# A kernel of attention and two expert stages: the products of packed keys for both halves of the heads, at one place in y

## The chip, the cores and the metric

The kernel runs on one core of a Trainium2 chip. Its engines are TensorE (PE: matmuls and their weight loads), VectorE (DVE), ScalarE (ACT), GpSimd (POOL) and SyncE (SP, which here issues the DMAs); each runs its own instructions in order and they wait for each other by semaphores. The metric is the device time of one execution in microseconds (us), as the median of runs.

## What is computed

Three steps follow one another; the third is the longest, and the change lies in the second.

```python
p_packed = sm_attn(p, k, v)                  # 8 batches, 8 heads, 32 packed queries, 576 keys of 64
x = sm_attn(q, p_packed, p_packed)           # 576 queries against the 32 packed rows
...
h = np.maximum(np.maximum(x @ w1, x @ w2), x @ w3)   # 4608 tokens, 512 -> 768
x2 = h @ w_out                                       # 768 -> 512
...
h = x2 @ w_in                                # 512 -> 2048, then P(h) / Q(h), elementwise
out = g @ w_out2                             # 2048 -> 512
```

## The kernel before

The kernel never forms x. Since x is the attention weights of a query (32 per head) times the packed rows, x @ w is those weights times (packed rows @ w), and the small products m = packed rows @ w are what the change moves.

The batches are worked in four batch pairs, bp0 to bp3. Each has a y-phase and an x2-phase:

- **y-phase.** Six slices f of the 768 hidden columns, 128 each, and two batches b2: `y_stage` (L462 ff.) makes three w-steps, one for each of w1, w2, w3, of 12 matmuls of 128 x 288. The first is copied out of PSUM by ACT (L471), the other two are joined with it by a max on DVE (L473). So a batch pair has 36 w-steps, counted here 0 to 35. After each, `between()` is called, which issues whatever else goes on beside y.
- **m.** `m_stage(bp, g, mt)` makes the products of one half g of the heads (four heads of each of two batches) with the columns of slice f + 1: eight matmuls of 32 output rows and 384 columns (L321) into one PSUM tile pst, a copy by ACT (L325) that gives the high part, and, in the function that it returns, a subtraction on DVE (L326) that gives the low part. It takes the next weight tile wt and, by `again(n)`, issues the DMA that fills another with a later piece of the same weights from the scratch w_scr. Both halves are needed when y comes to slice f + 1.
- **x2-phase.** Eight `x2_stage`, four output slices m of two batches: 36 matmuls into a PSUM tile psy, whose copy out is made by ACT (m under 3) or DVE (L489), and a store.
- **Weights.** They come packed in 64 bits and are decoded piece by piece (`Feed`): a load of w_raw on SP (L104), DVE L76, L82, ACT L83, L84, DVE L87, L91, L96, and POOL L99, which writes the wt tile; then a store of the decoded piece from SP to a scratch. In bp0 these are w1 to w3 and w_out; in bp1 to bp3 the weights of the third step.
- **Next batch pair.** Its attention (`Ahead`; scores S, transposes T, values V, scaling Z, query side s) runs in between, spread over the w-steps by the table PACK and over the x2-phase by SECOND, which holds the first slice's m.

Buffers that bind: two PSUM tiles pst (m, T, V and Z share them), two psy, four wt, three w_raw, one dec_r, and one pair of m tiles for even and one for odd slices.

The order of the instructions on each engine is made by a list scheduler: it has a simulated timeline and takes, engine by engine, the first instruction in the program's order whose inputs it holds for ready. So instructions can move ahead of the place where the code issues them, and one edit can change the order far from it. A few decode steps keep the program's order. The third step (moe2) follows after bp3.

Of the kernel before, what the change touches and what calls it, by code (L numbers as in the profile page):

```python
# [33 lines left out]
def attn_moe_moe2_kernel(  # L34
# [177 lines left out]
    def next_wt():  # L212

        n = next(used)
        wt = wt_ready.pop(n)
        n += NWT
        return wt, (n if NW <= n < NBP * NW else None)

    def again(n):
        if n is not None:  # L220
            wt = wt_tile().rearrange("p a b -> p (a b)")[:, :768]
            nc.sync.dma_start(wt, w_scr[n // 2 % 6, n % 2])
            wt_ready[n] = wt
# [21 lines left out]
    def load_w2(tiles, o, n):  # L245

        for x in range(2):
            nc.sync.dma_start(tiles[:, x].bitcast(F32), w2_scr[:, x, 512 * o : 512 * (o + n)])
# [58 lines left out]
    def m_tiles(f):  # L307

        return [mp[f % 2].tile([128, 2, 2, 384], F32R, name=f"m{x}") for x in "hl"]

    def m_stage(bp, g, mt):

        ps = ps_t.tile([128, 2, 512], F32, name="pst")
        wt, n = next_wt()
        for b2 in range(2):
            for h in range(4):
                i, j = divmod(h, 2)
                l, c = slice(64 * j, 64 * j + 64), 32 * (h ^ b2)  # L320
                pe.matmul(ps[c : c + 32, b2, :384], lhsT=ppk[l, bp % 2, 2 * g + b2, 32 * h : 32 * h + 32],  # L321
                          rhs=wt[l, 384 * i : 384 * i + 384], start=True, stop=True)
        again(n)
        hi, lo = (t[:, :, g, :] for t in mt)
        act.copy(hi, ps[:, :, :384])  # L325
        return lambda: dve.tensor_tensor(out=lo, in0=ps[:, :, :384], in1=hi.bitcast(F32), op=ALU.subtract)  # L326
# [132 lines left out]
    def y_stage(b2, f, m, a2, between, lo_eng):  # L459
        hm = hx.tile([128, 2, 288], F32, name="hm")  # L460
        mh, ml = m
        for w in range(3):  # L462
            ps = ps_y.tile([128, 2, 512], F32, name="psy")
            for half in range(2):
                for g in range(2):
                    ah, al = a2[g]
                    c = slice(288 * half, 288 * half + 288)
                    mm3(ps[:, half, :288], mh[:, g, 128 * w : 128 * w + 128], ml[:, g, 128 * w : 128 * w + 128],
                        ah[:, c], al[:, c], g == 0, g == 1)
            if w == 0:  # L470
              act.copy(hm, ps[:, :, :288])  # L471
            else:
              dve.tensor_tensor(out=hm, in0=ps[:, :, :288], in1=hm, op=ALU.max)  # L473
            between()
        hh = hp_pool.tile([128, S], F32R, name=f"hh{b2}{f}")
        hl = hp_pool.tile([128, S], F32R, name=f"hl{b2}{f}")
        split(hh, hl, hm.rearrange("p a b -> p (a b)"), lo_eng=lo_eng)
        return hh, hl
# [13 lines left out]
    def wi_at(f):  # L492

        if f < 1:
            return wi_0
        return wi_b[:, :, f - 1]
# [36 lines left out]
    for bp in range(NBP):  # L533
# [20 lines left out]
        for f in range(6):  # L554
            if f < 5:
                nmt = m_tiles(f + 1)

            def between(bp=bp, f=f, now=now):
                t = next(turn)
                if now.soft:  # L560
                    now.do("g")
                if f < 5 and t % 6 in (2, 4):
                    m_stage(bp, t % 6 // 2 - 1, nmt)()
                if t >= 2:
                    next(pack, None)
                if bp == 0:
                    if t % 3 < 2 and t < 32:
                        feed.half_step()
                elif t in y_steps[bp]:
                    feed2.step()  # L570

            if bp == NBP - 1 and f == 2:
                load_w2(wi_at(0), 0, 1)
            for b2 in range(2):
                hs[b2][f] = y_stage(b2, f, [t[:, b2] for t in mt], a2[b2], between,
                                    "dve" if bp == 0 or (b2, f) == (1, 5) else "pool")
            mt = nmt
# [109 lines left out]
    f = NQA  # L687
# [65 lines left out]
```

## Time and profile before

| | us |
|---|---|
| median of 3 runs | 1391.42 (1391.15 to 1391.81) |
| span of the profiled execution | 1386.2 |
| y-phase of bp0, from its first matmuls, and x2-phase | to 160.4, to 205.5 |
| bp1: y-phase, x2-phase | 85.1, 49.6 |
| bp2: y-phase, x2-phase | 85.2, 57.1 |
| bp3: y-phase, x2-phase | 67.5, 39.3 |
| moe2 | from 589.3 to the end |

The span is that of one profiled execution; it lies 5.2 us under the median of the runs, which have the start and the end of the execution around it. The page gives TensorE as busy for 1308.8 us (94% of the span), VectorE for 1055.0 and ScalarE for 802.8. The page's chain is read from the end back; the timelines give each instruction's start and duration, and in brackets how long its engine was idle before it and what ended that. PEclk is the granted clock of TensorE as a share of 2.4 GHz.

### The profile page before, as it was taken

The page shows a single profiled execution, that of the slowest core. Times are in us where ns is not written, and L with a number is a line of the kernel's source. Part 1 is how long each engine was busy: PE and PEld are TensorE (multiplying, and loading weights), DVE is VectorE, ACT ScalarE, POOL GpSimd, SP SyncE. Part 2 cuts the span into 40 slices and gives each one's busy share as a digit, 9 for nine tenths or more (in the row PEclk, how much of TensorE's full clock was granted, in tenths as well). Part 3 has the DMA queues.
Part 4 walks back from the last instruction along what each step waited for, and adds up shares of the span by engine and source line. Part 5 has one row for each costly group of instructions (what it writes and reads, how often), then busy time and mean ns, then how long its engine had stood idle before and what let it go on. Part 6 is the DMA issues. An engine that isn't in the chain of part 4 may idle for free.

```text
span 1386.2 us, 21521 instructions
## 1 busy us (share of the span) xinstructions
PE 1308.8 (94%) x8496; PEld 1089.6 (79%) x8496; DVE 1055.0 (76%) x1634; ACT 802.8 (58%) x1337; POOL 235.4 (17%) x226
## 2 busy tenths in 40 slices
PE   4488999999998899999999999999999999999998
PEld 2277787779777889988888888888888888888886
DVE  4698766677667764188888978889888888888887
ACT  2355534443443342276866867668677686776765
POOL 2332253334333533000100101001010010100000
PEclk8599999999999999999999999999999999999999
DMA  8567546666654731960100101001010010010000
GB/s 278 182 203 257 182 140 197 211 207 218 191 186 142 238 100 59 329 258 1 61 1 3 60 1 49 12 1 61 1 38 24 0 54 0 16 38 1 31 0 31
DMA packets 51557, 140.86 MB, mean 102 GB/s; under 512 B 5632, under 2 KB 5632, under 8 KB 50688
## 3 DMA queue, kind: packets, MB, share of 16 engines
q1 hardware_dynamic: 51168, 138.96, 30.2%
q8 instruction: 67, 1.10, 0.3%
q10 hardware_dynamic: 288, 0.52, 0.1%
q14 instruction: 34, 0.28, 0.1%
HBM read 99.09 MB, written 40.37 MB: 101 GB/s over the span
## 4 chain that ended last, share of the span: by engine, by line
PE 79%; DVE 7%; DMA 3%; ACT 2%; issue 2%; POOL 1%; SPq 0%; POOLq 0%; ACTq 0%; DVEq 0%
PE po L61 10%; PE po L62 10%; PE po L63 10%; PE psh L62 9%; PE psh L61 9%; PE psh L63 9%; PE psy L61 7%; PE psy L63 6%; PE psy L62 6%; PE pst L321 2%; DMA w_scr<-wt 1%; POOL wt L99 1%; DVE hm L473 1%; DMA w_raw<-in_w_dram 1%; DVE wt L91 1%
## 5 line engine op out<-in xcount | busy, mean ns | idle before, releaser
L61 PE MATMUL po<-wq_b,gh 128*128 128x512 f32 x540 | 212.3, 393 | 0.8 <-ACT gh L54 0.8
L62 PE MATMUL po<-wq_b,gh 128*128 128x512 f32 x540 | 211.3, 391 | 0.0
L62 PE MATMUL psh<-xl,wi_b 128*128 128x512 f32 x540 | 211.0, 391 | 0.0
L63 PE MATMUL psh<-xh,wi_b 128*128 128x512 f32 x540 | 210.6, 390 | 0.0
L61 PE MATMUL psh<-xh,wi_b 128*128 128x512 f32 x540 | 210.6, 390 | 0.0
L652 ACT ACTIVATE hb<-psh,babs 128x512 f32<-128x512 f32 (+1 forms) x145 | 100.1, 690 | 188.9 <-PE psh L63 188.9
L61 PE MATMUL psy<-a2h,mh 128*128 128x288 f32 x576 | 180.3, 313 | 11.5 <-DVE hm L473 6.1
L655 DVE SCALAR_TENSOR_TENSOR hb<-h,babs,hb 128x512 f32<-128x512 f32 (+1 forms) x145 | 108.3, 747 | 97.7 <-ACT h L653 97.5
L63 PE MATMUL po<-wq_b,gl 128*128 128x512 f32 x540 | 181.7, 391 | 0.0
L63 PE MATMUL psy<-a2h,ml 128*128 128x288 f32 x576 | 171.2, 298 | 4.6 <-DVE ml L326 4.6
L62 PE MATMUL psy<-a2l,mh 128*128 128x288 f32 x576 | 171.5, 298 | 0.0
L58 POOL TENSOR_TENSOR xl<-xr,xh 128x512 fp32r<-128x512 f32 x28 | 36.5, 1304 | 632.3 <-ACT xh L54 632.3
L61 PEld LDWEIGHTS psy<-a2h,mh 128*128 128x128 f32 x576 | 109.6, 190 | 36.2 <-DVE hm L473 11.2
L61 PE MATMUL psy<-hh,wo_h 128*128 128x288 f32 x384 | 117.6, 306 | 9.7 <-ACT hm L489 9.3
L63 PEld LDWEIGHTS po<-wq_b,gl 128*128 128x128 f32 x540 | 101.3, 188 | 24.0
L61 PEld LDWEIGHTS po<-wq_b,gh 128*128 128x128 f32 x540 | 101.4, 188 | 22.9 <-ACT gh L54 1.2
L62 PEld LDWEIGHTS po<-wq_b,gh 128*128 128x128 f32 x540 | 101.4, 188 | 22.4
L61 PEld LDWEIGHTS psh<-xh,wi_b 128*128 128x128 f32 x540 | 101.4, 188 | 22.1
L62 PEld LDWEIGHTS psh<-xl,wi_b 128*128 128x128 f32 x540 | 101.4, 188 | 21.7
L63 PEld LDWEIGHTS psh<-xh,wi_b 128*128 128x128 f32 x540 | 101.4, 188 | 21.7
L62 PE MATMUL psy<-hl,wo_h 128*128 128x288 f32 x384 | 115.8, 301 | 0.0
L63 PE MATMUL psy<-hh,wo_l 128*128 128x288 f32 x384 | 115.6, 301 | 0.0
(105 smaller groups left out, 2765.3 us busy)
## 6 DMA issues: line engine op xcount, KB each, us to landing
w_raw<-in_w_dram SPq DMA_DIRECT2D x32, 512.0 KB, 4.0
w_scr<-wt SPq DMA_DIRECT2D x32, 512.0 KB, 4.9
wt<-w_scr SPq DMA_DIRECT2D x36, 384.0 KB, 4.1
kt<-in_k_dram SPq DMA_DIRECT2D x16, 576.0 KB, 5.6
vraw<-in_v_dram SPq DMA_DIRECT2D x16, 576.0 KB, 6.6
kt<-in_q_dram SPq DMA_DIRECT2D x16, 576.0 KB, 5.6
w_raw<-in_w_dram SPq DMA_DIRECT2D x12, 768.0 KB, 5.6
x_scr<-hm SPq DMA_DIRECT2D x32, 288.0 KB, 4.1
```

What stands on the lines that cost most here:

```text
L58: e.tensor_tensor(out=lo, in0=src, in1=hi.bitcast(F32), op=ALU.subtract)
L61: pe.matmul(out_ap, lhsT=lh, rhs=rh, start=first, stop=False)
L62: pe.matmul(out_ap, lhsT=lh, rhs=rl, start=False, stop=False)
L63: pe.matmul(out_ap, lhsT=ll, rhs=rh, start=False, stop=last)
L91: dve.scalar_tensor_tensor(out=hib, in0=hw, scalar=-0x80000000, in1=t, op0=ALU.bitwise_and, op1=ALU.bitwise_or)
L99: pool.tensor_tensor(out=lo, in0=rf, in1=w.bitcast(F32), op=ALU.mult)
L321: pe.matmul(ps[c : c + 32, b2, :384], lhsT=ppk[l, bp % 2, 2 * g + b2, 32 * h : 32 * h + 32], rhs=wt[l, 384 * i : 384 * i + 384], start=Tru ...
L473: dve.tensor_tensor(out=hm, in0=ps[:, :, :288], in1=hm, op=ALU.max)
L652: act.activation(hb, h, AF.Abs, scale=babs[:, 0:1])
L655: dve.scalar_tensor_tensor(out=hb, in0=h2, scalar=babs[:, 1:2], in1=hb, op0=ALU.mult, op1=ALU.add)
```

## The change

In `between()`, w-step t of the batch pair: before, the products of half 0 come at t % 6 == 2 and those of half 1 at t % 6 == 4, each with its own copy and subtraction. After, both halves come at t % 6 == 2: eight products and their copy, eight products and their copy, and then the two subtractions. The place t % 6 == 4 is left with what it holds besides. It touches slices 0 to 4 of the four batch pairs, 20 times two stages; the first slice's products (in START and SECOND) are written as before.

```diff
--- before.py
+++ after.py
@@ -559,8 +559,9 @@
                 t = next(turn)
                 if now.soft:
                     now.do("g")
-                if f < 5 and t % 6 in (2, 4):
-                    m_stage(bp, t % 6 // 2 - 1, nmt)()
+                if f < 5 and t % 6 == 2:
+                    for low in [m_stage(bp, g, nmt) for g in range(2)]:
+                        low()
                 if t >= 2:
                     next(pack, None)
                 if bp == 0:
```

TensorE, bp1, steps 24 to 25 of the y-phase. L61 to L63 are y matmuls, L399 a transpose of the attention of bp2. Before:

```order
L61 MATMUL psy<-a2h_3527,mh 128x288
L62 MATMUL psy<-a2l_3528,mh 128x288
L63 MATMUL psy<-a2h_3527,ml 128x288
L399 MATMUL pst<-ident,zt_110 128x128
L61 MATMUL psy<-a2h_3446,mh 128x288
```

After:

```order
L61 MATMUL psy<-a2h_3527,mh 128x288
L62 MATMUL psy<-a2l_3528,mh 128x288
L63 MATMUL psy<-a2h_3527,ml 128x288
L321 MATMUL pst<-wt,ppk 32x384 x10
L61 MATMUL psy<-a2h_3446,mh 128x288
```

Where the transpose stood, ten products of m now stand in one row; the transpose comes later, at step 27.

VectorE, bp1, ahead of the max L473 of step 24 (psy_2954). L326 is the subtraction of m, L91, L96, L76 and L82 are decode steps. Before:

```order
L91 SCALAR_TENSOR_TENSOR wt_2968<-w_raw_2563,dec_t_2841 128x512
L96 TENSOR_SCALAR w_raw_2563<-wt_2968 128x512
L76 TENSOR_SCALAR dec_t_3097<-w_raw_2838 128x512
L370 RECIPROCAL sm_2903<-sm_2903 128x1
L326 TENSOR_TENSOR ml_2911<-pst_2996,mh_2910 128x2x384
L82 TENSOR_SCALAR dec_r_2977<-w_raw_2723 128x512
L473 TENSOR_TENSOR hm_2912<-psy_2954,hm_2912 128x576
```

After:

```order
L91 SCALAR_TENSOR_TENSOR wt_2846<-w_raw_2453,dec_t_2726 128x512
L96 TENSOR_SCALAR w_raw_2453<-wt_2846 128x512
L76 TENSOR_SCALAR dec_t_2976<-w_raw_2723 128x512
L326 TENSOR_TENSOR ml_2911<-pst_2996,mh_2910 128x2x384
L91 SCALAR_TENSOR_TENSOR wt_2968<-w_raw_2563,dec_t_2854 128x512
L326 TENSOR_TENSOR ml_2911<-pst_3008,mh_2910 128x2x384
L82 TENSOR_SCALAR dec_r_2855<-w_raw_2563 128x512
L473 TENSOR_TENSOR hm_2912<-psy_2954,hm_2912 128x576
```

A second subtraction and a second L91 have come ahead of the max, and the weight pieces behind them are one earlier.

ScalarE, x2-phase of bp1, around the second x2 copy (hm_3367). L325 is the copy of m, L83 and L84 are decode steps, L293 belongs to the attention. Before:

```order
L489 COPY hm_3283<-psy_3246 128x576
L325 CAST mh_3768<-pst_3827 128x2x384
L325 CAST mh_3768<-pst_3893 128x2x384
L293 ACTIVATE e_3310<-e_3310 128x576
L83 ACTIVATE dec_t_3479<-dec_t_3479,reb_70 128x512
L489 COPY hm_3367<-psy_3330 128x576
L84 ACTIVATE dec_r_3325<-dec_r_3325 128x512
```

After:

```order
L489 COPY hm_3283<-psy_3246 128x576
L84 ACTIVATE dec_r_3325<-dec_r_3325 128x512
L83 ACTIVATE dec_t_3612<-dec_t_3612,reb_70 128x512
L84 ACTIVATE dec_r_3480<-dec_r_3480 128x512
L293 ACTIVATE e_3310<-e_3310 128x576
L489 COPY hm_3367<-psy_3330 128x576
L83 ACTIVATE dec_t_3712<-dec_t_3712,reb_70 128x512
```

The two copies of m have left the place between the first and the second L489 (they now stand ahead of the first), and two L84 and another L83 have come in.

## Rows read from the trace of the kernel before

**Rows 1.** Page, chain that ended last, share of the span by engine.

```profile
PE 79%; DVE 7%; DMA 3%; ACT 2%; issue 2%; POOL 1%; SPq 0%; POOLq 0%; ACTq 0%; DVEq 0%
```

**Rows 2.** Windows, the stage moe2: length, busy us per engine, PEclk, DMA share, GB/s.

```profile
589.30:1386.00 796.70, 792.08 (x3456) 648.67 (x3456) 670.87 (x1019) 564.16 (x933) 36.53 (x28) 1.00 0.10 32
```

**Rows 3.** Timeline of PE: start us, us, operation, matmul records, [wait before].

```profile
289.19 1.51 PE L321 MATMUL pst<-wt,ppk 64*32 64x384 f32 x30
290.64 0.40 PE L61 MATMUL psy<-hh,wo_h 128*128 128x288 f32 x1
...
495.37 0.88 PE L321 MATMUL pst<-wt,ppk 64*32 64x384 f32 x16
496.17 0.40 PE L61 MATMUL psy<-a2h,mh 128*128 128x288 f32 x1
...
526.87 0.83 PE L321 MATMUL pst<-wt,ppk 64*32 64x384 f32 x2
527.63 0.40 PE L61 MATMUL psy<-a2h,mh 128*128 128x288 f32 x1
```

**Rows 4.** Waits of PE, y-phase of bp1: us in all, times, longest us.

```profile
PE psy L61 <- ACT e L359: 1.8, 1, 1.8
PE psy L61 <- DVE hm L473: 1.4, 2, 1.2
```

**Rows 5.** Waits of PE, x2-phases of bp1 (first row) and bp2.

```profile
PE psy L61 <- ACT hm L489: 3.6, 2, 3.4
...
PE psy L61 <- ACT hm L489: 3.5, 2, 2.2
PE pst L321 <- issue: 2.9, 1, 2.9
PE pst L321 <- DVE ml L326: 1.3, 1, 1.3
```

**Rows 6.** Windows of the x2-phases of bp0, bp1, bp2 and bp2; third last column PEclk.

```profile
186.00:192.00 6.00, 5.75 (x43) 5.75 (x44) 4.40 (x9) 2.53 (x5) 4.38 (x3) 1.00 0.31 125
310.00:320.00 10.00, 7.52 (x36) 7.50 (x36) 9.73 (x17) 4.34 (x8) 5.96 (x5) 0.66 0.87 297
436.00:450.00 14.00, 9.76 (x79) 7.16 (x78) 12.15 (x19) 3.28 (x5) 6.65 (x5) 0.76 0.43 139
450.00:463.00 13.00, 9.74 (x86) 8.01 (x84) 12.70 (x21) 5.79 (x10) 6.52 (x6) 0.87 0.85 279
```

**Rows 7.** Timeline of ACT, x2-phase of bp1.

```profile
309.29 0.72 ACT L83 ACTIVATE dec_t<-dec_t,reb 128x512 int32<-128x512 int32 x1 [4.77 <-DVE dec_t L76]
...
311.81 0.62 ACT L489 COPY hm<-psy 128x576 f32<-128x576 f32 x1
```

**Rows 8.** Timeline of DVE, x2-phases of bp1 and bp2.

```profile
308.38 0.82 DVE L76 TENSOR_SCALAR dec_t<-w_raw 128x512 int32<-128x512 int32 x1 [1.37 <-DMA w_raw<-in_w_dram]
...
437.72 0.69 DVE L91 SCALAR_TENSOR_TENSOR wt<-w_raw,dec_t 128x512 int32<-128x512 int32 x1 [5.65 <-DMA w_scr<-wt]
```

**Rows 9.** Groups by line and shape: count, busy us, mean ns, idle before, releasers.

```profile
L473 DVE TENSOR_TENSOR hm<-psy,hm 128x576 f32<-128x576 f32 x96 | 72.3, 753 | 56.8 <-PE psy L63 51.6 <-PE pst L377 2.2 <-ACT hm L471 2.1
...
L326 DVE TENSOR_TENSOR ml<-pst,mh 128x768 fp32r<-128x768 f32 x48 | 45.2, 948 | 5.9 <-ACT mh L325 5.6
L99 POOL TENSOR_TENSOR wt<-dec_r,w_raw 128x512 fp32r<-128x512 f32 x32 | 43.0, 1343 | 46.2 <-DVE w_raw L96 29.3 <-DVE dec_r L87 7.9 <-issue 5.8
L325 ACT CAST mh<-pst 128x768 fp32r<-128x768 f32 x48 | 37.7, 798 | 20.6 <-PE pst L321 11.5 <-PE psy L62 8.8
...
L87 DVE SCALAR_TENSOR_TENSOR dec_r<-w_raw,dec_r 128x512 f32<-128x512 uint32 x32 | 31.7, 992 | 8.9 <-ACT dec_r L84 8.6
...
L91 DVE SCALAR_TENSOR_TENSOR wt<-w_raw,dec_t 128x512 int32<-128x512 int32 x32 | 25.9, 808 | 15.8 <-DMA w_scr<-wt 11.6 <-PE pst L321 3.6
...
L84 ACT ACTIVATE dec_r<-dec_r 128x512 f32<-128x512 int32 x32 | 20.2, 631 | 25.0 <-DVE dec_r L82 25.0
```

**Rows 10.** Timeline of PE, x2-phase of bp0, after a wait.

```profile
186.25 0.40 PE L61 MATMUL psy<-hh,wo_h 128*128 128x288 f32 x1 [2.26 <-ACT hm L489]
```

## The prediction

> **What bounds the kernel now.** (bp0 to bp3 are the four batch pairs.) I read the chain first: four fifths of the span runs along TensorE [rows 1]. Then the windows by stage. From 589 us to the end (moe2) TensorE is busy for 792.08 of 796.70 us [rows 2], and the order of every instruction there is the same in both kernels, so nothing can be gained or lost in that part. What the change can move lies between 73 us, where the first y-phase is running, and 589 us. There too TensorE is the bound, so the time moves for three reasons only: TensorE gets other work (the visits to the m products), TensorE waits for something else, or its clock is granted differently.
>
> The third view is TensorE's timeline around the m products [rows 3]. A row of it counts two matmul records for each product. A visit of eight products (x16) holds the y matmuls up from 495.37 to 496.17, 0.80 us; a visit of one product (x2) from 526.87 to 527.63, 0.76 us; a visit of fifteen (x30) from 289.19 to 290.64, 1.45 us. The eight products of a stage run side by side, so a visit is paid by whole streams: 0.8 us for anything up to eight products, 1.45 us for nine to sixteen. What matters is into how many visits the products fall, not how many products there are.
>
> The fourth view is what TensorE waits for. In the y-phase of bp1 the two waits that matter are 1.8 us for the exponentials and 1.2 us for the max on VectorE [rows 4]; bp2 repeats them within 0.1 us. In the x2-phases the waits are 3.6 us in bp1 and 3.5 + 2.9 + 1.3 = 7.7 us in bp2 [rows 5], and around them the granted clock averages 0.66 over 10 us, 0.76 over 14 us and 0.87 over 13 us [rows 6]. The clock has two levels, 1.2 and 2.4 GHz, so these are 6.8, 6.7 and 3.4 us at the lower one.
>
> Where the x2 waits come from is read on the two engines behind them. The next x2 step needs the PSUM tile that ScalarE's copy L489 empties. In bp1 that copy starts at 311.81, behind a decode activation (L83) that idled 4.77 us for VectorE [rows 7], which in turn idled for the raw weights to land at 308.38 [rows 8]. In bp2 VectorE stood 5.65 us, until 437.72, in front of a decode step (L91) whose target tile was still being stored [rows 8]. So the x2 waits are the decoding of weights at the head of in-order queues, not the m products as such.
>
> **The change part by part.**
>
> *What it does to the order.* In the code both products now come at the first place. In the order of instructions it is otherwise: the products already run up to a slice ahead of the code, as soon as their weights are ready, and the second half is never what y waits for in either kernel. In the order of the changed kernel only some pairs end up together. Counted from 73 us on, the m products of bp0 to bp3 fall into 15, 11, 13 and 9 visits before, of which 0, 2, 3 and 1 hold more than eight products; after, into 14, 14, 16 and 8, of which 2, 2, 3 and 2 hold more.
>
> *Visits on TensorE.* At 0.80 and 1.45 us [rows 3]: bp0 from 15 x 0.80 = 12.0 to 12 x 0.80 + 2 x 1.45 = 12.5, +0.5; bp1 from 9 x 0.80 + 2 x 1.45 = 10.1 to 12 x 0.80 + 2.9 = 12.5, +2.4; bp2 from 10 x 0.80 + 4.35 to 13 x 0.80 + 4.35, +2.4; bp3 from 7.85 to 7.7, -0.15. Sum **+5.2 us**, all on TensorE and so on the path, unless a visit stands where TensorE would have waited. Ends: +2.5, if half of them do; +6.5, if each further visit also costs the slower restart of the y matmuls behind it.
>
> *Waits in the y-phase.* The 1.8 us for the exponentials [rows 4] are covered after, since ten products stand in front of the matmul that waited: 0. The max L473 of step 24 now stands behind two subtractions L326 and two decode steps L91 instead of one of each. With the rows' own durations the two subtractions, the max and the copy in front of them are 2 x 0.95 + 0.75 + 0.80 = 3.5 us [rows 9], and the decode rows between make it 5 to 6; TensorE has a visit of 1.45 us and two y steps to do meanwhile. I follow the order by hand to a wait of 2.3 us where it was 1.2. So per bp2.3 against 3.0, for bp1 and bp2 together **-1.4 us**. Ends: 0 wait each (-6.0) and a wait of 5.65 each, as VectorE's longest before L91 [rows 8] (+5.3). Bp0 has the same orders on VectorE, GpSimd and the queues but for a few neighbours swapped: 0, with 2 us either way.
>
> *The x2-phase of bp1.* The products for the next batch pair's first slice and one decode piece go ahead of the x2-phase, and the load of one raw piece, issued before behind the first store of x2 on SP's queue, is issued ahead of it. The 1.37 us of VectorE for that load go, and with them the long idle of L83. But between the first and the second copy L489 ScalarE now has two L84 with L83 and L293, where it had two copies L325, L293 and L83: one more hop through VectorE and GpSimd. A piece costs 0.63 + 0.99 + 1.34 = 3.0 us on L84, L87 and L99 [rows 9], and the next cannot start its own before that (one dec_r tile). Following that by hand I get a wait of 2.2 us at the second x2 step and 1.5 at the third: 3.7 where 3.6 stood. What I expect to go is the low clock: of its 6.8 us about 6.0 fell on matmuls, which cost half of that, 3.0 us. A wait of 2.26 us at 186.25 [rows 10] was followed by a clock of 1.00 [rows 6]. So 6.6 becomes 3.7, **-2.9 us**. Ends: all of it gone (-6.6), and waits and clock as before plus one more piece (+3.0).
>
> On the same question the Trainium skill (TensorE: Matmul & The Clock Gate, section "A second HAM failure mode: psum-queue depth-cycling") says that frequent short idling between groups of matmuls can also make the clock swing between its levels. The row at 186.25 speaks against it, but it is a single wait. By that rule the two short waits of bp1 would keep the 3.0 us.
>
> *The x2-phase of bp2.* The same move, but here the order puts the decode piece that waits for a store later, before the third step: by hand 2.2 us at the second step, 3.8 at the third, and the low clock after the longer one, 3.0. Before: 7.7 of waits and, of 10.1 us at the low clock, about 7 with matmuls, 3.5. So 11.2 becomes 9.0, **-2.2 us**. Ends -11.2 and +3.
>
> *Sum.* 5.2 - 1.4 - 2.9 - 2.2 = -1.3 us on a span of 1386.2. The median, 1391.4, has 5.2 us around the span, which stay. Forecast 1391.4 - 1.3 = **1390.1 us**. What this measurement can tell from no change is 0.2%, 2.8 us.
>
> **The rivals.**
>
> *Faster: the x2 waits go for good.* If the earlier raw load and the earlier release of the weight tiles take the stalls of bp1 away with their low clock (-6.6) and leave bp2 only a wait of 3 us without low clock (-8.2), the sum is 5.2 - 1.4 - 6.6 - 8.2 = -11: 1380; with half of the gain in bp2, 1384. I take 1383. For it: both x2 stalls began with DMA, and the change brings both transfers forward. Against it: ScalarE's queue has more decode rows in front of the second copy than before.
>
> *Slower: VectorE's queue holds the max up.* Price and place: the L473 of step 24 in bp1 and bp2. If the store that frees the tile of the second L91 in front of it lands later than TensorE's two y steps and the visit last, L473 waits as L91 did at 437.72, 5.65 us, and TensorE with it: 3.4 us more per batch pair than I took, 6.7 in all, and 1390.1 + 6.7 = 1396.8. For it: two decode steps and both subtractions now stand there together. Against it: of the 11.6 us that L91 waited for stores in the whole kernel [rows 9], half is that one place in the x2-phase of bp2.
>
> *The clock still falls in bp1.* The 3.0 us stay: 1390.1 + 3.0 = 1393.1; the skill's sentence above is on this side. For it: the waits come closer together than at 186.25.
>
> *It does what it says: all pairs adjacent.* A pair in one visit costs 1.45 in place of 1.60, and over the 20 pairs that is 3.0 us less, in place of the 5.2 more: 1390.1 - 8.2 = 1381.9. The order speaks against it plainly, most pairs are split by the pool of two tiles and by other products.
>
> **How the numbers follow.** Forecast 0.33, faster rival 0.28, clock 0.14, slower rival 0.22, adjacent pairs 0.03. The forecast spreads by some 3 us (same 0.23, faster 0.06, slower 0.04); the clock case falls half within and lies half beyond 0.2% above (same 0.09, slower 0.05); the faster rival ends within 0.2% in one case of ten (same 0.03). Faster 0.06 + 0.25 + 0.03 = 0.34, same 0.35, slower 0.31. The range must reach into both rivals and the ends of the x2 terms: **1382 to 1399**; the forecast's own is 1387 to 1393.5.
>
> **What would show it.** Visits: in the profile after, 52 groups of L321 behind 73 us instead of 48, and TensorE busier by about 5 us between 73 and 589. Y-phase: the wait for the exponentials near step 27 gone, one for L473 of about 2.3 us. X2-phase of bp1: two waits for L489, 1.5 to 2.2 us each, and PEclk 1.00; were it 0.66 again, the clock step is wrong. Bp2: a wait of near 4 us before the third step with PEclk below 1. It is wrong altogether if y stages stretch by more than 5 us per batch pair, or if an x2-phase shows a wait above 4 us.

## The result: 11 us slower

| | median, us | runs from to | ratio to before, 95% interval |
|---|---|---|---|
| before | 1391.62 | 1391.15 to 1392.76 | |
| after | 1402.60 | 1396.66 to 1404.84 | 1.0084, 1.0064 to 1.0105 |

The forecast was 1390.1 us, no difference, with a range that ended at 1399. The changed kernel is slower by 0.84%, some 11 us, and lies above the range. Over the later runs before has a median of 1389.8 to 1390.7 and its single runs spread from 1384.7 to 1394.0, more widely than the first three showed. The profiled execution of before (span 1386.2) took less than those three: over 71 later runs the time lies only 1.8 us above the span, not 5.2, so that execution was a run of some 1388, and most of the 5.2 us that were taken for the start and the end of the execution are the difference between two executions. The profiled execution after has a span of 1399.4, 13.2 us more, and the stages show where.

The page's chain after, shares of the span by engine, beside [rows 1]:

```profile
PE 80%; DVE 11%; DMA 3%; POOL 2%; ACT 2%; issue 2%; SPq 0%; POOLq 0%; ACTq 0%; DVEq 0%
```

The share of VectorE has gone from 7 to 11% of the chain, the share of TensorE from 79 to 80%. The windows of the stages after, from bp0's x2-phase to bp3's (window, its length, busy us of PE, PEld, DVE, ACT and POOL with counts, PEclk, DMA share, GB/s):

```profile
162.42:209.65 47.23, 44.69 (x379) 41.24 (x374) 29.49 (x46) 17.69 (x26) 20.68 (x14) 0.96 0.42 142
209.65:300.87 91.22, 86.72 (x910) 69.32 (x909) 58.05 (x95) 38.62 (x71) 28.71 (x35) 0.98 0.56 177
300.87:352.77 51.90, 44.87 (x355) 42.08 (x353) 39.18 (x61) 18.36 (x29) 24.69 (x18) 0.93 0.73 244
352.77:442.26 89.49, 85.28 (x911) 68.04 (x909) 58.60 (x95) 38.61 (x71) 28.81 (x35) 1.00 0.50 158
442.26:494.37 52.11, 45.65 (x387) 41.63 (x385) 37.09 (x61) 18.32 (x29) 23.89 (x18) 0.93 0.64 213
494.37:563.26 68.89, 67.11 (x530) 59.51 (x529) 41.51 (x60) 25.56 (x40) 24.51 (x17) 1.00 0.25 85
563.26:602.55 39.29, 38.35 (x290) 38.14 (x289) 7.33 (x11) 8.68 (x14) 0.00 (x0) 1.00 0.89 316
```

Against the table of before, by the first matmul of each stage: bp0's x2-phase 45.0 to 47.2, bp1 85.2 + 49.5 to 91.2 + 51.9, bp2 85.2 + 57.0 to 89.5 + 52.1, bp3's y-phase 67.6 to 68.9, its x2-phase the same. Bp0's y-phase ends 2.0 us later, and moe2 has the same length. So bp1 lost 8.4 us, bp2 gained 0.7, bp0 lost 4.2 and bp3 1.3: 13.2 in all.

TensorE's waits after, in the y-phase of bp1, beside [rows 4] (us in all, times, longest):

```profile
PE psy L61 <- DVE hm L473: 2.3, 2, 2.1
PE pst L377 <- ACT e L359: 1.3, 1, 1.3
PE pst L377 <- DVE ml L326: 0.8, 1, 0.8
```

The wait for the exponentials in front of y (1.8 us) is gone, as predicted. The one for L473 is longer, 2.1 us, but it stands near step 14 and not at step 24; and 0.8 us for a subtraction L326 is new, in front of a transpose (L377). The 1.3 us in front of L377 stand in before too. In the x2-phases of bp1 and then bp2, beside [rows 5]:

```profile
PE psy L61 <- ACT hm L489: 7.0, 4, 2.9
...
PE psy L61 <- ACT hm L489: 6.2, 2, 4.5
```

In bp1 four waits of 7.0 us stand where two of 3.6 stood; in bp2 6.2 where 7.7 stood.

What these waits are is read on the engines behind them. VectorE and then TensorE, y-phase of bp1 (start, us, operation, [idle before, and what ended it]):

```profile
243.80 0.43 DVE L76 TENSOR_SCALAR dec_t<-w_raw 128x512 int32<-128x512 int32 x1 [1.56 <-DMA w_raw<-in_w_dram]
244.15 0.95 DVE L326 TENSOR_TENSOR ml<-pst,mh 128x768 fp32r<-128x768 f32 x1
245.01 0.75 DVE L473 TENSOR_TENSOR hm<-psy,hm 128x576 f32<-128x576 f32 x1
...
245.82 0.40 PE L61 MATMUL psy<-a2h,mh 128*128 128x288 f32 x1 [2.11 <-DVE hm L473]
```

A decode step L76 waits 1.56 us for its raw weights to land; queued behind it on VectorE are the subtraction L326 and the max L473, and TensorE waits 2.11 us for the latter. The x2-phase of bp1: ScalarE and then TensorE at the first and the last of the four waits; then VectorE's row for the second wait, its row for the first, and the rows of VectorE and GpSimd for the last:

```profile
307.70 0.72 ACT L83 ACTIVATE dec_t<-dec_t,reb 128x512 int32<-128x512 int32 x1 [2.12 <-DVE dec_t L76]
308.33 0.62 ACT L489 COPY hm<-psy 128x576 f32<-128x576 f32 x1
...
330.78 0.68 ACT L293 ACTIVATE e<-e 128x576 f32<-128x576 f32 x1 [1.60 <-POOL e L291]
331.37 0.62 ACT L489 COPY hm<-psy 128x576 f32<-128x576 f32 x1
...
309.00 0.61 PE L61 MATMUL psy<-hh,wo_h 128*128 128x288 f32 x1 [2.44 <-ACT hm L489]
...
332.04 0.40 PE L61 MATMUL psy<-hh,wo_h 128*128 128x288 f32 x1 [2.87 <-ACT hm L489]
...
312.93 1.33 DVE L76 TENSOR_SCALAR dec_t<-w_raw 128x512 int32<-128x512 int32 x1 [0.84 <-DMA w_raw<-in_w_dram]
...
307.19 0.42 DVE L76 TENSOR_SCALAR dec_t<-w_raw 128x512 int32<-128x512 int32 x1
...
326.69 1.67 DVE L76 TENSOR_SCALAR dec_t<-w_raw 128x512 int32<-128x512 int32 x1
328.28 0.74 DVE L290 TENSOR_REDUCE mx<-e 128x18 f32<-128x576 f32 x1
...
329.10 1.65 POOL L291 TENSOR_TENSOR e<-e,mx 128x576 f32<-128x576 f32 x1 [1.02 <-DVE mx L290]
```

TensorE waits for the copy L489 each time, and in front of the copy stand, in ScalarE's order, L83, which waits for VectorE's L76, or L293, which waits for GpSimd's L291 and so for VectorE's L290. Only at the second wait, 0.65 us, does that L76 itself wait for a load (0.84 us). Ahead of the first wait VectorE works from 301.21 to 307.6 us without a pause, two subtractions L326 among it, after 0.60 us for a load; ahead of the third and the fourth it works from 315.63 to 333 us without a pause. So in three of the four waits ScalarE is late because VectorE is busy. On SP's queue, from 285 to 334 us, the raw loads L104 wait in turn for the decode three pieces earlier, since there are three raw tiles; in the same stretch of before they wait for 9.6 us:

```profile
SPq L104 <- POOL wt L99: 21.1, 7, 8.4
```

### The profile page after: what moved, and what is told of

The parts are those of the page before. It is cut to its first block, busy times and chain, and to the rows that moved or that the text cites. A ratio compares the mean times of both kernels' runs of the same rounds, so it can differ in the third digit from the quotient of the medians.

```text
span 1399.4 us, 21536 instructions
## 1 busy us (share of the span) xinstructions
PE 1317.7 (94%) x8496; PEld 1093.8 (78%) x8496; DVE 1058.7 (76%) x1634; ACT 802.9 (57%) x1337; POOL 233.8 (17%) x226
## 4 chain that ended last, share of the span: by engine, by line
PE 80%; DVE 11%; DMA 3%; POOL 2%; ACT 2%; issue 2%; SPq 0%; POOLq 0%; ACTq 0%; DVEq 0%
PE po L61 9%; PE po L63 9%; PE po L62 9%; PE psh L62 9%; PE psh L61 9%; PE psh L63 9%; PE psy L61 7%; PE psy L63 6%; PE psy L62 6%; DMA w_raw<-in_w_dram 2%; PE pst L321 2%; DVE ml L326 1%; DVE hm L473 1%; DVE dec_t L76 1%; POOL wt L99 1%
## 5 line engine op out<-in xcount | busy, mean ns | idle before, releaser
L61 PE MATMUL po<-wq_b,gh 128*128 128x512 f32 x540 | 212.3, 393 | 0.8 <-ACT gh L54 0.8
L63 PE MATMUL psh<-xh,wi_b 128*128 128x512 f32 x540 | 210.6, 390 | 0.0
L61 PE MATMUL psh<-xh,wi_b 128*128 128x512 f32 x540 | 210.6, 390 | 0.0
L653 ACT ACTIVATE hb<-psh,babs 128x512 f32<-128x512 f32 (+1 forms) x145 | 100.2, 691 | 188.9 <-PE psh L63 188.9
L61 PE MATMUL psy<-a2h,mh 128*128 128x288 f32 x576 | 181.9, 316 | 12.4 <-DVE hm L473 9.8
L63 PE MATMUL po<-wq_b,gl 128*128 128x512 f32 x540 | 181.7, 391 | 0.0
L63 PE MATMUL psy<-a2h,ml 128*128 128x288 f32 x576 | 172.3, 299 | 5.3 <-DVE ml L326 5.3
L61 PEld LDWEIGHTS psy<-a2h,mh 128*128 128x128 f32 x576 | 110.8, 192 | 44.4 <-DVE hm L473 15.5
L61 PE MATMUL psy<-hh,wo_h 128*128 128x288 f32 x384 | 117.7, 307 | 16.0 <-ACT hm L489 15.6
L63 PEld LDWEIGHTS po<-wq_b,gl 128*128 128x128 f32 x540 | 101.3, 188 | 24.0
L61 PEld LDWEIGHTS po<-wq_b,gh 128*128 128x128 f32 x540 | 101.4, 188 | 22.9 <-ACT gh L54 1.2
L61 PEld LDWEIGHTS psh<-xh,wi_b 128*128 128x128 f32 x540 | 101.4, 188 | 22.1
L63 PEld LDWEIGHTS psh<-xh,wi_b 128*128 128x128 f32 x540 | 101.4, 188 | 21.7
L473 DVE TENSOR_TENSOR hm<-psy,hm 128x576 f32<-128x576 f32 x96 | 72.2, 753 | 60.3 <-PE psy L63 53.5
```

Source lines behind the costliest of these rows:

```text
L61: pe.matmul(out_ap, lhsT=lh, rhs=rh, start=first, stop=False)
L63: pe.matmul(out_ap, lhsT=ll, rhs=rh, start=False, stop=last)
L653: act.activation(hb, h, AF.Abs, scale=babs[:, 0:1])
```

## The experiments

Theories after the result. **Queues:** the new order has put decode steps, which wait for loads, stores and each other, in front of L473 and L489. **Streams:** the products take more streams of TensorE (rows of up to eight products side by side), as predicted. **Togetherness:** two stages in a row by themselves (both pst tiles, two copies, two subtractions) hold up what lies beside them. A second question is where in the program the loss arises: in all slices alike, in those in which the products are moved past a feed step (a step of the decoding), or in bp0. Times of these runs are against before on the same chip, 1389.8 to 1390.7 us. Where I name "PE time in the visits", it is the sum over all interruptions of y and x2 of the time from the last big matmul before to the first one behind, less the waits and that matmul's own 0.13 us: 89.8 us in before, 95.3 in after. Where I say that two kernels have the same order in a stage, every engine's instructions, by line and tile name, follow one another there alike in the two profiles.

### The subtractions' place in the code

```diff
-                    for low in [m_stage(bp, g, nmt) for g in range(2)]:
-                        low()
+                    for g in range(2):
+                        m_stage(bp, g, nmt)()
```

> Both halves at the first place, but each product's subtraction written straight behind it instead of both behind both products. Every engine's instructions stand in the same order as in the changed kernel, so this is the changed kernel again. All theories: +9 to +13 us against before (1400 to 1405). What its second profile is for: the waits of TensorE (2.1 us for L473 near step 14 of bp1, 4.5 us for L489 in the x2-phase of bp2, four waits for L489 in bp1) should recur within 0.3 us at the same places, because the order sets them; the stretches at the lower clock may fall elsewhere, and the spread of the runs (some 8 us) should go with the mean clock, which the queues do not explain.

Measured 1401.47 us, ratio 1.0080 (1.0059 to 1.0101). With the same order the loss is the same: the scheduler makes the same program of either text, so writing the two subtractions behind both products has no effect, and this run is the changed kernel once more. In the second profile PE time in the visits is 95.2 us, and in bp1's x2-phase the waits for L489 stand at the same steps (2.46, 1.08 and 2.87 us beside 2.44, 1.07 and 2.87). In bp2 the two waits are 3.27 and 1.89 where they were 1.73 and 4.52, so "within 0.3" held for bp1 (the 2.11 is 1.83) and not for bp2's x2-phase. The spread of the runs does not go with the mean clock either: over 71 runs of before the two are correlated with 0.15.

### Which slices: past a feed step or not

```diff
-                if f < 5 and t % 6 in (2, 4):
+                if bp > 0 and f in (1, 3):
+                    if t % 6 == 2:
+                        for low in [m_stage(bp, g, nmt) for g in range(2)]:
+                            low()
+                elif f < 5 and t % 6 in (2, 4):
                     m_stage(bp, t % 6 // 2 - 1, nmt)()
```

This is against the kernel before, and the other kernel has `(0, 2, 4)` for `(1, 3)`. The edits of the further runs on slices have the same shape, and only their first changed line is shown.

> The change in slices 1 and 3 of bp1 to bp3 alone: these are the pairs whose second product was written behind a feed step (w-steps 9 and 21) and is now written ahead of it, so that the product's next weight tile and the decoded piece swap their turn in the ring of four wt tiles. Theory of the ring and the queues (decode steps come to wait in front of L473 and L489): this carries most of the loss, +5 to +9 us. Rival (the loss comes from the products standing together: visits, both pst tiles, two subtractions in a row): 6 of the 20 pairs moved, +3 us. Rival (bp0): 0.

> The change in slices 0, 2 and 4 of bp1 to bp3 alone: no feed step lies between the two places, the ring of wt tiles keeps its turns. Theory of the ring: within 2.5 us of before. Rival (products together): 9 of the 20 pairs moved, +4 to +6 us, more than the slices 1 and 3 alone. Rival (bp0): 0.

Measured 1387.64 us, 0.9984 (0.9972 to 0.9995), for slices 1 and 3, and 1391.59, 1.0011 (0.9997 to 1.0025), for slices 0, 2 and 4. My theory of the ring fell: the slices that move past a feed step make the kernel faster by 2 us. Togetherness as such falls with it, since six pairs written together cost nothing. PE time in the visits is 90.3 us with slices 1 and 3 and 92.7 with 0, 2 and 4, where before has 89.8; both together, with bp0 left alone, 95.1. So the parts don't add: 0.5 and 2.9 make 5.3 when done together. In the x2-phase of bp1 either part has the order of the changed kernel, and the waits for L489 are there with 8.0 us (slices 1 and 3) and 7.1: they stand in a kernel that is faster than before, so these waits alone are not the loss. That kernel makes up for them elsewhere: TensorE waits 1.8 us in each y-phase of bp1 and bp2 where it waits 4.4 in before, and the x2-phase of bp2 is 52.6 us long.

### Bp0 and the rest

```diff
-                if f < 5 and t % 6 in (2, 4):
+                if bp == 0:
+                    if f < 5 and t % 6 == 2:
...
```

The second kernel of this pair has `if f < 5 and bp > 0:` and under it `if t % 6 == 2:`.

> The change in bp0 alone, whose feed has another rhythm (half steps at two of three w-steps). The profile of the changed kernel has bp0 longer by 2.0 us in the y-phase and 2.2 us in the x2-phase, of which 1.7 us each is a stretch at the lower clock. Theory of the queues: +1 to +4.5 us, by whether the lower clock recurs. Rival (products together): 5 of the 20 pairs, +2 to +3 us. If the clock stretches of bp0 were chance and not the order's doing: +0.5 us.

> The change in all slices of bp1 to bp3, bp0 as before. With the change in bp0 alone at +3.5 us, the parts add up if this is at +7 to +8 us. Theory now held: three sources, 5.5 us of TensorE time for the products in more streams (5.4 of it in bp1 and bp2), about 4 us of waits and lower clock in bp0, some 2 us of waits in bp1 to bp3; so +7 us here and bp0's stages as before. Rival (bp0's change moves what follows, for instance the turn of the wt tiles at the start of bp1): clearly less than +6 or the stages of bp1 differ from those of the changed kernel by over 1 us.

Measured 1393.71 us, 1.0025 (1.0013 to 1.0038), with bp0 alone, and 1397.02, 1.0050 (1.0029 to 1.0071), without it: 3.9 and 7.2 us, together 11.1, which is the loss of the whole change (11.0 and 11.6 in its two series of runs); bp1's stages without the change in bp0, 91.2 and 51.9 us, are those of the changed kernel to 0.1 us. Bp0, for which the prediction had 0.5 us of visits and no waits, is a third of it. In the profiles the y-phase of bp0 takes 100.3 to 100.6 us in all seven kernels that leave bp0 alone (from its first matmul; the ninth product below is not counted), and 102.2 to 104.5 in all five that bring its products to the first place, with 6.8 to 9.7 us at the lower clock in the former and 13.0 to 14.6 in the latter. Most of the difference lies at two waits. From 74 to 160 us the seven have no stretch at the lower clock; with bp0 alone changed there are two, of 3.4 us each, at waits of 2.87 and 2.0 us that end at 101.9 and 127.9 us. Windows, first with slices 1 and 3, then twice with bp0 alone (third last column PEclk):

```profile
73.00:160.00 87.00, 77.78 (x882) 62.47 (x864) 78.78 (x116) 49.76 (x82) 25.73 (x27) 1.00 0.67 226
...
101.00:106.00 5.00, 4.07 (x27) 3.26 (x28) 2.55 (x5) 1.40 (x2) 0.00 (x0) 0.66 0.40 162
127.00:133.00 6.00, 5.08 (x38) 4.41 (x39) 2.66 (x5) 2.27 (x3) 0.87 (x1) 0.72 0.53 198
```

The five have one or two such stretches; in the changed kernel's own profile only the second is there. Where matmuls fill one, it costs half of its 3.4 us, an estimate of 1.7 us each. The wait that grew most with bp0 alone changed, in rows of VectorE, GpSimd and TensorE:

```profile
98.58 0.55 DVE L76 TENSOR_SCALAR dec_t<-w_raw 128x768 int32<-128x768 int32 x1
99.04 2.17 DVE L80 TENSOR_SCALAR dec_r<-w_raw 128x768 int32<-128x768 int32 x1
101.13 0.74 DVE L473 TENSOR_TENSOR hm<-psy,hm 128x576 f32<-128x576 f32 x1
...
98.63 2.17 POOL L99 TENSOR_TENSOR wt<-wt,dec_t 128x768 f32<-128x768 f32 x1 [2.62 <-DVE dec_t L91]
...
101.93 0.61 PE L61 MATMUL psy<-a2h,mh 128*128 128x288 f32 x1 [2.87 <-DVE hm L473]
```

L473 now stands behind L76 and L80, and L80, which takes 0.55 us in other places, takes 2.17 while L99 runs on GpSimd; both end within 0.5 us of each other. In before, too, four of the ten L80 in bp0 take 1.8 us, each begun 0.4 to 0.5 us after an L99, while two that begin 0.2 us ahead of an L99 take 0.55; there no L473 that TensorE waits for this long is behind a slow one. TensorE waits 2.87 us where its longest wait for L473 in this stage was 1.16, and its next matmul takes 0.61 us instead of 0.40. The Trainium skill (SBUF — State Buffer, section "SBUF: two separate sides") tells of a port pair that GpSimd shares with VectorE for some of VectorE's instructions, and that the one that starts first holds for its whole instruction; the rows agree in that L80 ends 0.4 us behind L99, but no run here took L99 away.

Which slice makes that order:

```diff
-                if f < 5 and t % 6 in (2, 4):
+                if bp == 0 and f == 0:
...
```

> The change in slice 0 of bp0 alone. In bp0 alone changed, TensorE waits 2.87 us for L473 near 102 us, where before it waits 1.16; L473 then stands behind L91, L76 and L80, and L80 takes 2.17 us beside GpSimd's L99 in place of 0.55. Of the orders with one slice changed, only this one has that row of VectorE. Theory: the wait of 2.8 to 2.9 us is here, and no 2.0 us near 127; +0.5 to +2.5 us. Rival (it takes several slices): wait of 1.2 us as before and no difference.

Measured 1391.18 us, 1.0007 (0.9996 to 1.0018). The wait is there with one slice:

```profile
99.53 2.17 DVE L80 TENSOR_SCALAR dec_r<-w_raw 128x768 int32<-128x768 int32 x1
101.62 0.74 DVE L473 TENSOR_TENSOR hm<-psy,hm 128x576 f32<-128x576 f32 x1
...
102.42 0.61 PE L61 MATMUL psy<-a2h,mh 128*128 128x288 f32 x1 [2.38 <-DVE hm L473]
```

It is 2.38 us and not 2.8 to 2.9, there is none of 2.0 us near 127, but one of 2.03 for the exponentials at 119.6. In the time it can't be told from nothing (-0.6 to +2.5 us). So slice 0 accounts for that wait. Whether it accounts for the 3.9 us of bp0 alone is open: by the median of ten runs it does not, but in its one profile bp0 takes 104.5 + 46.6 us, as long as with bp0 alone (103.2 + 47.3), with two stretches of 3.4 us at the lower clock. Which of the other slices adds what was not run.

### The loads

In both kernels, the raw pieces of the third step's weights behind the first three are not loaded; the decoding takes what lies in the three tiles:

```diff
-                self.raw.append((load_raw(self.pl, piece[1], self.bufs), piece))
+                if piece[1].shape[1] > 512 or len(self.kept) < self.bufs:
+                    raw = load_raw(self.pl, piece[1], self.bufs)
+                    if piece[1].shape[1] == 512:
+                        self.kept.append(raw)
+                else:
+                    self.kept.append(self.kept.pop(0))
+                    raw = self.kept[-1]
+                self.raw.append((raw, piece))
```

> The changed kernel without the raw loads of the third step's weights after the first three pieces (each later piece decodes what lies in the tile; 29 loads of 512 KB left out, all engines' instructions stay). VectorE's L76 then never waits for a load. Theory (decode steps that wait for their load stand in front of the x2 copies): TensorE's waits for L489 in bp1, 6.9 us, fall under 2, the 1.8 to 2.1 us near step 14 of bp1 and bp2 go, the stretches at the lower clock with them, and the time falls by 10 to 16 us against the changed kernel. Rival (the copies are late because ScalarE and VectorE have too much to do there): the waits for L489 stay above 5 us and the time falls by less than 4.

> The kernel before without the same loads. Theory: bp1's wait of 3.4 us goes, bp2's wait for a store (2.9 us and what follows) stays or shrinks, -5 to -10 us against before; the distance to the changed kernel without loads is then the products' streams and bp0, 8 to 10 us. Rival: less than 3 us faster, and the distance stays at 11 to 12.

Measured 1386.42 us for after without the loads (0.9976 of before, 0.9964 to 0.9988), 15 us less than after with them, and 1377.88 for before without them (0.9914, 0.9893 to 0.9935), 12 less, where 5 to 10 had been expected. Waits of TensorE in after without the loads, x2-phase of bp1 and then its y-phase (the lines are 7 higher: L496 is L489, L480 is L473):

```profile
PE psy L61 <- ACT hm L496: 2.1, 1, 2.1
...
PE pst L384 <- ACT e L366: 1.3, 1, 1.3
PE pst L384 <- DVE ml L333: 0.8, 1, 0.8
PE psy L61 <- DVE hm L480: 0.7, 2, 0.4
```

The 7.0 us for L489 are 2.1, and the 2.1 for L473 is 0.4. In before without the loads, x2-phase of bp1:

```profile
PE psy L61 <- ACT hm L496: 4.6, 3, 2.2
```

So without the loads most of the waits for L489 go from the changed kernel. For L473 the rows above show the load that it stood behind. For L489 the way is not shown: the scheduler, which reckons with the loads, has also put VectorE and ScalarE in another order (in this x2-phase 22 of VectorE's 61 instructions and 7 of ScalarE's 29 stand elsewhere or in another stage, TensorE's none), and VectorE is busy there for 34.5 us in place of 39.2. So the lateness of the loads and the order of the decode steps changed together. In before the single wait of 3.4 us has gone, but three of 4.6 us in all have come. The loads cost both kernels more than 10 us; what the change adds through them is the difference of the distances, 11 to 12 with loads and 8.5 without, some 3 us. That the 8.5 that stay are the streams and bp0 is read from the two profiles, where PE time in the visits differs by 6.5 us, bp0 by 5.2 and the x2-phase of bp1 by -2.3; no run takes them apart.

### What a visit costs

In the kernel before, a ninth product in each stage:

```diff
+        pe.matmul(ps[:32, 0, :384], lhsT=ppk[:64, bp % 2, 2 * g, :32], rhs=wt[:64, :384], start=True, stop=True)
         again(n)
```

> The kernel before with a ninth matmul in each product stage: the first of the eight once more into the same place, the output is unchanged. 46 stages behind 73 us. Theory (a visit is paid by streams of eight side by side): each stage costs a second stream, 46 x 0.65 = +30 us, less what falls into waits, so +20 to +32. Rival (a product costs its share, 0.80 / 8): 46 x 0.1 = +5 us.

Measured 1414.21 us, 1.0164 (1.0150 to 1.0178): +23.5 us, 0.51 us a stage, and 26.8 us more PE time in the visits, 0.58 a stage. A visit in the y-phase of bp3 (L323 is the ninth, x counts two records each):

```profile
520.37 0.88 PE L321 MATMUL pst<-wt,ppk 64*32 64x384 f32 x16
521.03 0.81 PE L323 MATMUL pst<-wt,ppk 64*32 64x384 f32 x2
521.77 0.40 PE L61 MATMUL psy<-a2h,mh 128*128 128x288 f32 x1
```

From 520.37 to 521.77 are 1.40 us, where eight took 0.80 [rows 3]. One product more costs 0.60 us, six times its share of a stage. The price of the sum is right: a visit is paid by streams of eight.

### The second place, and slice 1

```diff
-                if f < 5 and t % 6 == 2:
+                if f < 5 and t % 6 == 4:
```

> Both halves together at the second place (t % 6 == 4) in place of the first. The orders of VectorE and ScalarE differ little from those of the changed kernel (408 and 334 lines against over 2,000 to before). If the loss hangs on the products standing together in the program, and so in the ring of tiles: +9 to +13 us, as the changed kernel. If it hangs on the first place (earlier demand for the weights): +2 to +6.

Measured 1393.29 us, 1.0027 (1.0015 to 1.0039): +2.6 us, a quarter of the loss, though the code moves the products just as close together and PE time in the visits is even higher, 97.6 us. What it saves is waits. Those of the y-phase of bp1:

```profile
PE pst L377 <- ACT e L359: 1.6, 3, 1.2
PE psy L61 <- DVE hm L473: 0.2, 1, 0.2
```

1.8 us where after has 4.4, and bp0's y-phase takes 100.2 us, as in before, and has the clock of before. About half of what it saves is bp0 (145.3 us for 149.4 in the profiles). The x2-phase of bp1 has the order of the changed kernel and waits of 8.0 us for L489. So neither togetherness nor the streams alone nor those waits make the loss; most of the difference between the two places lies in bp0 and in the y-phase of bp1, where the orders of VectorE and ScalarE differ.

```diff
-                if f < 5 and t % 6 in (2, 4):
+                if bp > 0 and f == 1:
...
```

> The change in slice 1 of bp1 to bp3 alone. Counted from the order, the products of bp1 and bp2 keep the streams of before or lose one, and the first slice's products of the next batch pair stay in the x2-phase. The kernel with slices 1 and 3 was 2.2 us faster than before. If that gain comes from slice 1 (fewer streams): -1 to -3 us here. If it comes from the x2-phase, which only slice 3 changes: within 1 us of before, and x2 of bp2 at 55 to 57 us.

Measured 1389.58 us, 1.0000 (0.9986 to 1.0013). Slice 1 alone gives nothing that can be told. Bp2's x2-phase takes 54.5 us, against 57.0 in before and 52.6 with slices 1 and 3; but the kernels with bp0 alone and with its slice 0 alone, which have before's order in all of bp1 and bp2, give 55.1 and 54.6. So a stage of the same order differs by up to 2.4 us from one execution to another, and the 57.0 is the longest of three. PE time in the visits is 87.9 us, 1.9 less, which the time doesn't show.

### A version that is faster than both

Put together from the stages of these runs:

```diff
-                if f < 5 and t % 6 in (2, 4):
+                if (bp, f) in ((1, 1), (2, 1), (2, 3)):
...
```

> The change in slice 1 of bp1 and in slices 1 and 3 of bp2 alone, put together from stage lengths: bp1 as with slice 1 alone (84.9 + 47.6 us), bp2 as with slices 1 and 3 (84.9 + 52.6), bp0 and bp3 as before. If stages add up: bp1 -2.2 against the profile of before, bp2 -4.8, so -4 to -7 us, faster than both kernels. If a stage's length depends on what the stage before left in the queues and rings: -2 to +1 us.

Measured 1385.28 us, 0.9957 (0.9943 to 0.9970): 5.4 us faster than before and 17 faster than the change. Its windows of bp1 (y, x2) and bp2 (y, x2):

```profile
207.05:293.40 86.35, 80.65 (x892) 67.01 (x891) 54.71 (x93) 38.17 (x71) 28.91 (x34) 1.00 0.56 181
293.40:342.65 49.25, 45.84 (x376) 42.36 (x372) 39.36 (x64) 19.34 (x30) 25.06 (x18) 0.93 0.80 268
342.65:427.50 84.85, 83.10 (x910) 67.50 (x908) 58.25 (x95) 38.30 (x71) 29.34 (x35) 1.00 0.51 168
427.50:479.40 51.90, 45.41 (x388) 41.39 (x385) 42.31 (x66) 19.73 (x31) 26.05 (x19) 0.97 0.67 232
```

Bp2 is as foretold, 84.9 and 51.9 us for 142.3 before, -5.5; against the two other executions with before's order of bp2, 141.8 and 139.8 us, it is -5.0 and -3.0. Bp1 is not: 86.4 and 49.3 in place of 84.9 and 47.6, though it has the order of the kernel with slice 1 alone. In the x2-phase that order is also before's, which gives 49.2 to 49.6 us in three profiles: the 47.6, with 3.4 us at the lower clock in place of 6.8, was a lucky execution to build on. The gain is bp2's, whose first-slice products have left its x2-phase.

## Why the prediction was wrong, step by step

In short: the price of the visits was right, 5.5 us for 5.2. The rest, foretold as -6.5 us, came out as +7.0: in bp0, which was put at nothing, and in the x2-phase of bp1, which was to gain.

- **Visits, +5.2 us: right.** PE time in the visits rose by 5.5 us (5.4 in the second profile), L321 stands in 52 groups for 48, as foretold, and the ninth product bears out the price of a stream.
- **Waits in the y-phase, -1.4 us: wrong, as place and as size.** The idle time of TensorE is 4.4 us in bp1 as before and 4.1 for 4.45 in bp2. The 1.8 us for the exponentials went as predicted, and the 1.2 for L473 at step 24, which were to become 2.3, went too. In their place came L473 near step 14 (2.1 and 1.85 us) behind an L76 that waits for its load, and 0.8 us for a subtraction. I had followed VectorE's order at the place where a wait stood before, and not where the raw tiles run out.
- **Bp0, 0 with 2 either way: wrong, 3.9 us.** I had read "a few neighbours swapped" as nothing. In the y-phase of bp0 25 of VectorE's 131 instructions and 21 of ScalarE's 88 stand elsewhere; one of the moves put L80 in front of L473 while GpSimd writes a weight tile, and the clock falls at the longer waits.
- **X2-phase of bp1, -2.9 us: the term that was furthest off.** The waits rose from 3.6 to 7.0 us, and the low clock that was to go stayed (6.8 us, as before): +3.5, 6.4 off. The step that failed is the reading of [rows 7] and [rows 8], that with the 1.37 us for the load the long idle of L83 goes too. L83 idled 4.77 us, of which VectorE waited 1.37 for the load; the rest it worked. The two waits that I had counted by hand came at their steps, 2.4 and 0.7 us for 2.2 and 1.5. Two more came before the fourth and the fifth step, 1.1 and 2.9 us, where VectorE works without a pause; there five of its decode rows take 1.2 to 1.7 us, begun while GpSimd works, where others of these lines take 0.4 to 0.7. Without the loads the waits fall to 2.1, so the loads have a part in it, but whether by their lateness (L104 waits for the decode of three pieces before) or by the order that the scheduler makes with them stays open; no run had a fourth raw tile.
- **The clock after short waits: wrong.** I had concluded from one row [rows 10] that a wait of 2.26 us leaves the clock alone. The same wait stands in bp0's x2-phase in 13 of the profiles, 2.26 to 2.30 us each. The changed kernel, on TensorE's timeline:

```profile
188.91 0.40 PE L61 MATMUL psy<-hh,wo_h 128*128 128x288 f32 x1 [2.27 <-ACT hm L489]
```

Its window around that (third last column PEclk):

```profile
188.00:194.00 6.00, 5.09 (x27) 5.09 (x27) 4.69 (x9) 2.52 (x5) 3.73 (x3) 0.72 0.38 137
```

And the timeline with slice 1 alone changed:

```profile
186.16 0.40 PE L61 MATMUL psy<-hh,wo_h 128*128 128x288 f32 x1 [2.29 <-ACT hm L489]
```

Its window around that:

```profile
185.00:191.00 6.00, 4.84 (x36) 4.84 (x37) 4.93 (x9) 2.53 (x5) 3.48 (x3) 1.00 0.40 142
```

In nine of them the granted clock is then at 1.2 GHz for 3.4 us, in four it is not. The Trainium skill (TensorE: Matmul & The Clock Gate, section "A second HAM failure mode: psum-queue depth-cycling") says that frequent short idling between groups of matmuls makes the clock swing between its levels; the nine profiles are on its side, though here it is a single wait. The case of "the clock still falls in bp1" was the true one; it was worth 3.0 us and could not have made the 11.

- **X2-phase of bp2, -2.2 us: right in sign and size, in part by luck.** Waits 7.7 to 6.2, low clock 10.2 to 6.8 us (-1.7), so -3.2; over three profiles of either order the mean of waits and half the low clock differs by -2.3. The foretold wait of 3.8 us with low clock before the third step is there with 4.5. But the decode piece that was to wait for a store idles VectorE by 0.7 us only; ahead of that wait VectorE works.
- **Bp3, nothing but visits: 1.4 us missed.** It is one wait for L473 at 530.9, again behind an L76 that waits 0.92 us for its load.
- **The rivals.** The slower one had the mechanism nearly right, a decode step at the head of VectorE's queue in front of L473, but waiting for a store at step 24 where it was a load near step 14, and it had no ScalarE side. The faster one, that earlier loads would remove the x2 waits, did not come. With the terms as measured the sum is 5.5 + 3.9 + 3.5 - 3.2 + 1.4 - 0.3 + 1.7 (low clock behind the 2.1 us in bp1, which the second profile lacks) = 12.5, of 13.2 in the two profiles. Two terms lie beyond the ends that I had given them, bp0 by 2 us and the x2-phase of bp1 by half a us. The ends of all terms together reached to +20 us against before; the range drew them in to +7.6, as if gains and losses of the stages were independent.

What stays open: which slices of bp0 make its 3.9 us, how the loads bring about the waits in the x2-phase of bp1, why the streams of bp1 and bp2 grow by more than their parts, and what makes single runs of the same kernel differ by up to 9 us, beyond the clock that falls or not behind the same wait.

## What to carry to other kernels

When a change makes a scheduler reorder a whole program, the price of the moved work is the easy part of the sum. Here the wrong result came from what is queued in front of the instructions that free a PSUM tile. List for each of them, in every stage, the instructions ahead of it, and split the idle time in front of it: how long did the engine before it wait for a transfer, and how long did it work? Only the first part can go when the transfer comes earlier (here 1.37 of 4.77 us). Don't leave a stage out because few instructions seem to move. Take a stage's length from more than one profile: the same order gave 54.6 to 57.0 us. And apply such a change slice by slice: of 20 places three gave 5.4 us, all together cost 11.

## What was not expected of the hardware

- The same wait of 2.26 to 2.30 us before the same matmul is followed by a granted clock of 1.2 GHz for 3.4 us in nine profiles and not at all in four.
- A VectorE instruction of 0.55 us (L80, 128 x 768) takes 1.7 to 2.2 us where it starts while GpSimd's L99 runs.
- Eight products of 64 x 32 weights and 384 columns take 0.80 us of TensorE, one takes 0.76 and nine take 1.40.
